# Agent attention and a gated convolution on one core: TensorE's opening steps in a written order, a query load behind the values, value products in 32-column tiles

## The chip, the cores and the metric

One core of a Trainium2 chip runs the kernel. The metric is the device time of one execution in microseconds (us). The engines are TensorE (PE in the profile; its weight loads are PEld), VectorE (DVE), ScalarE (ACT), GpSimd (POOL) and SyncE (SP), which here only issues transfers.

## What is computed

Four batches, 12800 positions, 128 channels, 49 agents. The agents attend to all keys and gather the values; every query then attends to the agents; the result goes through a causal five-tap gate, a value product and an output product.

```python
def sm(a, b):
    s = scale * (a @ b.transpose(0, 2, 1))
    s = s - s.max(-1, keepdims=True)
    e = np.exp(s)
    return e / (e.sum(-1, keepdims=True) + 1e-09)
agent_v = sm(agents, k) @ v
x = sm(q, agents) @ agent_v
...
for k in range(K):
    gate_pre += conv_w[k][None, None, :] * xp[:, k:k + S, :]
gate = 1.0 / (1.0 + np.exp(-gate_pre))
val = x @ w_val
return (gate * val @ w_out).astype(np.float32)
```

## The kernel before

Positions are cut into 10 units of 1280 for each batch, and into 25 chunks of 512 for the second half. The kernel never forms x: it folds `agent_v` into the convolution and value weights, and applies these to the normalised query scores, which stand with agents on partitions in `x1`.

The names of the steps, used all through this text (b is the batch, u the unit, t the chunk, counted over all batches):

- **k b.u** (`key_scores`): eight float32 products of 32 columns by 320 (L363), written to one of two PSUM buffers `sc`; ScalarE copies them out (L389), VectorE takes the largest (L398). The four products of a half stand at the array's columns 0, 32, 64 and 96.
- **m0 and m1** (`key_max`, two steps each): the largest score of every agent; without it no exponential of the values can start.
- **v b.u** (`agent_values`): exponentials on ScalarE (L455), a block transpose on VectorE (L373), and ten float32 products of 64 columns by 129 (L463), alternating between columns 0 and 64. All units of a batch add up in the PSUM buffer `av`.
- **f1 to f5** (`fold_weights`, five steps in a row): f1 sums and normalises (`av` copied at L491, products L494 and L498, VectorE to `avT` at L508), f2 is a small product (L536), f3 eight transposes of the finished gate and value weights (L593, result `stat`), f4 one transpose (L629), f5 two (L655, result `wo16`). Between them VectorE, ScalarE and GpSimd do the scalings.
- **q b.u** (`queries`): the same eight products as k (L363), then a block transpose (L373), a maximum (L679), a subtraction on GpSimd (L684), exponentials on ScalarE (L692), sums and a scaling on VectorE (L697 to L706), and a split into float16 halves on ScalarE and GpSimd (L713 to L726).
- **t b.u** (`transposes`): the query weights to `x1`. For the first four units TensorE does it with ten transposes (L757), ScalarE and VectorE copy one half each (L764, L769); later units go by DMA. Behind it `shifts` copies five shifted pieces to `x2` by DMA (L791); for the very first unit ScalarE's queue issues two of the five.
- **g t, a t, o t** (`gates`, `values`, `project`): six, two and three float16 products of 128 columns by 512 (L828 and L832, L855 and L859, L898 to L900) in one PSUM bank each (`gate`, `val`, `out`).

The list `work` (L943 to L989) holds the steps in program order, and that is TensorE's order. For the other engines `Plan.order` picks, by estimated costs and the longest tail of work behind each step, what runs next. Loads of 640 KB go through a ring of 11 buffers `ld`, in the order in which `work` uses them; SyncE's queue issues them and most other transfers, strictly one after the other. The agents' table `ag_sb` is that queue's first transfer, the weights `moe` its second (L257, L326).

In `work` before the change stand ten keys, both key-maximum steps, q0.0 and q0.1, ten value units with t0.0 behind the eighth, then f1, k1.0, f2, k1.1, f3, two more keys, chunk 0, and so on with chunks and units in turn.

Of the kernel before, what the change touches and what calls it, by code (L numbers as in the profile page):

```python
# [19 lines left out]
BLK = 32  # L20
AP_ = 64

UNIT = 1280
NBLK = 10
# [17 lines left out]
EARLY = ((1, 4), (2, 5), (4, 6))  # L42
SINGLE = 4
KEYS_EARLY = 2
KEYS_FIRST = 2
AV0 = 4
PE_FIRST = 4
PE_TURNS = ()
TURN = 3
Q_FIRST = 2  # L50
W_AT = 2
T_AT = 7
HOP = 0.09
BACKLOG = 3.0
LANES = 8
# [7 lines left out]
class Plan:  # L63
# [11 lines left out]
    def add(self, engine, us, fn, reads=(), writes=(), moved=0.0, key=None, urge=0.0):  # L75
        i = len(self.steps)
        need = set()
        for x in reads:
            need |= self.wrote.get(x, set())
        for x in writes:  # L80
            need |= self.wrote.get(x, set()) | self.read.get(x, set())
        for x in reads:
            self.read.setdefault(x, set()).add(i)
        for x in writes:
            self.wrote[x], self.read[x] = {i}, set()
        self.steps.append((engine, us, fn, need, moved, key))
        self.urge.append(urge)
# [84 lines left out]
def tile_agent_attention_gated_conv(  # L172
# [9 lines left out]
    nc = tc.nc  # L182
    B, C, N = qT.shape
    A = 49
    NU = N // UNIT
# [4 lines left out]
    VW = NBLK * (C + 1)  # L190
    HB = NBLK // 2
# [4 lines left out]
    add = plan.add  # L196
# [60 lines left out]
    nc.sync.dma_start(out=ag_sb, in_=agT.rearrange("b c a -> c b a"))  # L257
    make_identity(nc, ident)
    make_identity(nc, ident16)
    nc.vector.tensor_tensor(  # L260
# [88 lines left out]
    def load(kind, b, u):  # L349
        i = taken[0] % NLOAD  # L350
        taken[0] += 1
        slot_of[kind, b, u] = i
        if kind == "v":
            dst, src = ld[i], vP[b, u].rearrange("p n c -> p (n c)")
        else:
            dst = ld[i][:, 0:UNIT]
            src = (kT if kind == "k" else qT)[b, :, u * UNIT : (u + 1) * UNIT]
        add("dma", 0.4, lambda: nc.sync.dma_start(out=dst, in_=src), (), [("ld", i)], 1.57)

    def score_matmuls(b, src, out):  # L360
        for j in range(2):
# [17 lines left out]
    def key_scores(b, u):  # L379
        i = slot_of["k", b, u]  # L380
        ps, at = bank()
        km = ("kmx", b % 2)
        add("pe", 1.07, lambda: score_matmuls(b, ld[i], ps), [("ld", i)], [at], key="sc")
# [64 lines left out]
    def agent_values(b, u):  # L448
        e, et = es[u % 2], ets[u % 3]
        i = slot_of["v", b, u]  # L450
        vt = ld[i].rearrange("p (n c) -> p n c", c=C + 1)

        def exps():
            for j in range(2):
                nc.scalar.activation(  # L455
                    out=e[:, j], in_=ks[:, u, j], func=AF.Exp,
                    bias=kbias[b % 2][:, j : j + 1], scale=SCALE,
                )

        def matmuls():  # L460
            for n in range(NBLK):
                o = (n % 2) * AP_
                nc.tensor.matmul(  # L463
                    out=av[o : o + AP_, 0 : C + 1], lhsT=et[:, n, :], rhs=vt[:, n, :],
                    start=(u == 0 and n < 2), stop=(u == NU - 1 and n >= NBLK - 2),
                )
# [3 lines left out]
        add(  # L470
            "pe", 1.07, matmuls, [("eT", u % 3), ("ld", i)], ["av"], key="av"
        )


    av2 = const.tile([P, C + 1], F32, name="av2")
# [191 lines left out]
    def queries(b, u):  # L667
        g = b * NU + u
        x = g % 2
        i = slot_of["q", b, u]  # L670
        ps, at = bank()
        sT, d, e, w, r, sm = sts[x], qw[g % 3], qw[g % 3], qw[g % 3], qr[x], qsm[x]
        pt = pts[g % 3]
        sa = sT[:, :, 0:A]
        add("pe", 1.07, lambda: score_matmuls(b, ld[i], ps), [("ld", i)], [at], key="sc")
# [26 lines left out]

        add("dve", 0.95, sums, [("qw", g % 3)], [("qr", x)])
        add(
            "dve", 0.68,
            lambda: nc.vector.tensor_tensor(  # L706
                out=w, in0=e, in1=r.unsqueeze(2).to_broadcast([P, NBLK, A]), op=ALU.mult
            ),
            [("qw", g % 3), ("qr", x)], [("qw", g % 3)],
        )  # L710
# [13 lines left out]
        add(  # L724
            "pool", 1.09,
            lambda: nc.gpsimd.tensor_tensor(  # L726
                out=pt[:, :, A : 2 * A], in0=w, in1=pt[:, :, 0:A], op=ALU.subtract
            ),
            [("qw", g % 3), (*p_, 0)], [(*p_, 1)],
        )  # L730
# [219 lines left out]
    work += [("fold", 0), ("k", 1, 0), ("fold", 0), ("k", 1, 1), ("fold", 0)]  # L950
    after = {
        0: [("fold", 0), ("q", 0, 2), ("fold", 0), ("t", 0, 1), ("q", 0, 3)],
        1: [("t", 0, 2)],
        2: [("t", 0, 3)],
    }
    before = {t: [] for t in range(NT + 2)}
# [5 lines left out]
    for b in range(B):  # L962
        t0 = b * NCH
        for i in range(NU):
            g = b * NU + i + LEAD
            if EARLY[-1][1] < g < B * NU:
                before[t0 + at[i]].append(("q", g // NU, g % NU))
                behind[t0 + at[i] + 2].append(("t", g // NU, g % NU))
        if b + 1 < B:
            u0 = KEYS_FIRST if b == 0 else KEYS_EARLY  # L970
            part = (NU - u0 + 3) // 4
            for n, u in enumerate(range(u0, NU)):
                before[t0 + at[n // part]].append(("k", b + 1, u))
            for t in MAX_AT:
                behind[t0 + t].append(("max", b + 1))
            for u in range(NU):
                before[t0 + at[AV0 + u // 2]].append(("v", b + 1, u))
            for i in range(5):
                behind[t0 + at[AV0 + 4] + i].append(("fold", b + 1))
            if b + 2 < B:  # L980
                for u in range(KEYS_EARLY):
                    before[t0 + at[NU - 1]].append(("k", b + 2, u))
    for t in range(len(chunks) + 2):
        work += before.get(t, [])
        if t < len(chunks):
            work += [("g", t), ("a", t)] + after.get(t, [])
        if t >= 2:
            work.append(("o", t - 2))
        work += behind.get(t, [])  # L989

    loads = [w for w in work if w[0] in "qkv"]

# [65 lines left out]
```

## Time and profile before

| | |
|---|---|
| median of 3 runs (lowest to highest) | 431.86 us (431.13 to 434.68) |
| the profiled execution, its own time | 431.22 us |
| its span | 429.4 us |
| TensorE busy within the span | 402.9 us |
| VectorE, ScalarE, GpSimd busy | 297.0, 300.4, 224.3 us |
| mean granted clock of TensorE | 0.996 |

How to read it: a row of the timeline gives the start, the length, the engine, the line, the operation with its output and inputs, the tile of the array, the shape and the count of merged instructions; in brackets stands how long the engine had been idle before it and whose end released it. TensorE's instructions overlap, so the length of a row holds the last one's tail, and the step from one row's start to the next one's is the better measure. A wait of TensorE is time at the end only while TensorE is the engine that sets the end.

### The profile page before, as it was taken

What the parts mean: (1) busy time and instruction counts of PE and PEld (TensorE: products, weight loads), DVE (VectorE), ACT (ScalarE), POOL (GpSimd) and SP (SyncE); (2) the same over time, 40 slices, a digit from 0 to 9 for tenths busy, and PEclk for the clock granted to TensorE, in tenths of its full rate; (3) what the DMA queues carried; (4) which work ended last, traced back from release to release, by engine and by line L of the source; (5) the groups of instructions that cost most, each with busy time, mean ns of one, the idle gap of its engine ahead of it and who ended that gap; (6) DMA issues with size and microseconds to landing.
All of it is one profiled execution on the core that took longest, in us unless ns stands there. A gap on an engine that the chain in (4) does not pass through costs nothing.

```text
span 429.4 us, 8968 instructions
## 1 busy us (share of the span) xinstructions
PE 402.9 (94%) x3307; PEld 194.8 (45%) x3307; DVE 297.0 (69%) x555; ACT 300.4 (70%) x520; POOL 224.3 (52%) x239
## 2 busy tenths in 40 slices
PE   3978888999999999999999999999999999999995
PEld 1357333345565444444555544445555544434443
DVE  3776879886786877578666887678666787566231
ACT  1464536678976577778876676778876577777875
POOL 1002246564466665544557665553356466687553
PEclk9999989999999999999999999999999999999999
DMA  8999999999999999999999999999999999887743
GB/s 288 422 415 415 371 350 337 297 285 309 343 358 294 249 270 289 307 309 305 340 329 356 292 323 292 320 312 334 306 330 257 289 291 287 215 199 173 192 156 122
DMA packets 76158, 128.07 MB, mean 298 GB/s; under 512 B 51644, under 2 KB 51900, under 8 KB 76116
## 3 DMA queue, kind: packets, MB, share of 16 engines
q1 hardware_dynamic: 76056, 127.41, 96.0%
q8 instruction: 26, 0.43, 0.4%
q14 instruction: 16, 0.13, 0.1%
q10 hardware_dynamic: 60, 0.10, 0.1%
HBM read 79.25 MB, written 26.21 MB: 246 GB/s over the span
## 4 chain that ended last, share of the span: by engine, by line
PE 65%; DMA 13%; DVE 12%; ACT 5%; issue 3%; SPq 1%; POOL 1%; DVEq 0%; ACTq 0%; POOLq 0%
PE gate L828 20%; PE sc L363 13%; PE av L463 6%; PE gate L832 4%; PE val L855 4%; PE val L859 4%; PE out L898 4%; PE out L899 4%; PE out L900 4%; DMA ld<-qT 3%; DMA ld<-vP 3%; DVE h L868 2%; ACT e L455 2%; DMA ld<-kT 2%; DMA outT<-ob 2%
## 5 line engine op out<-in xcount | busy, mean ns | idle before, releaser
L879 POOL TENSOR_TENSOR hl<-h,hh 128x512 f16<-128x512 f32 (+1 forms) x101 | 117.0, 1160 | 121.3 <-ACT hh L874 113.7
L828 PE MATMUL gate<-x,stat 128*128 128x512 f16 (+1 forms) x500 | 124.4, 378 | 2.4 <-ACT th L841 2.3
L868 DVE SCALAR_TENSOR_TENSOR h<-th,val 128x512 f32<-128x512 f32 x100 | 67.7, 677 | 69.1 <-PE out L899 46.1
L363 PE MATMUL sc<-ld,ag_sb 128*32 128x320 f32 x1280 | 102.0, 452 | 10.0 <-DMA ld<-kT 8.0
L912 ACT ACTIVATE ob<-out,oscale 128x512 f32<-128x512 f32 x98 | 67.2, 686 | 23.5 <-PE out L900 17.4
L841 ACT ACTIVATE th<-gate,unscale 128x512 f32<-128x512 f32 x100 | 68.3, 683 | 19.7 <-PE gate L832 18.0
L828 PEld LDWEIGHTS <-stat 128*128 128x128 f16 x505 | 45.6, 97 | 66.4 <-issue 19.0
L874 ACT CAST hh<-h 128x512 f16<-128x512 f32 (+1 forms) x101 | 61.4, 608 | 13.1 <-DVE h L868 12.4
L684 POOL TENSOR_TENSOR qw<-sT,qmx 128x490 f32<-128x490 f32 x40 | 41.5, 1038 | 50.2 <-DVE qmx L679 50.1
L363 PEld LDWEIGHTS sc<-ld,ag_sb 128*32 128x32 f32 x1280 | 37.0, 112 | 62.8 <-issue 22.5
L463 PE MATMUL av<-ld,eT 128*64 128x129 f32 x800 | 49.5, 275 | 1.7 <-DMA ld<-vP 1.4
L389 ACT COPY ks<-sc 128x640 f32<-128x640 f32 x40 | 27.7, 691 | 32.7 <-PE sc L363 30.6
L463 PEld LDWEIGHTS av<-ld,eT 128*64 128x64 f32 x800 | 43.7, 136 | 11.7 <-issue 7.3
L726 POOL TENSOR_TENSOR pt<-qw,pt 128x490 f16<-128x490 f32 x40 | 44.7, 1119 | 3.8 <-ACT pt L713 3.1
L455 ACT ACTIVATE e<-ks,kbias 128x320 f32<-128x320 f32 x80 | 39.0, 553 | 6.1 <-DVE kbias L444 3.3
L373 DVE STREAM_TRANSPOSE eT<-e 128x640 f32<-128x640 f32 x40 | 33.6, 842 | 11.4 <-ACT e L455 5.9
L373 DVE STREAM_TRANSPOSE sT<-sc 128x640 f32<-128x640 f32 x40 | 33.3, 834 | 10.8 <-PE sc L363 10.6
L398 DVE TENSOR_REDUCE kmx<-ks 128x2 f32<-128x640 f32 x39 | 31.4, 817 | 11.8 <-ACT ks L389 11.8
L832 PE MATMUL gate<-x,stat 100*128 100x512 f16 x100 | 38.0, 380 | 0.8 <-DMA x<-x 0.8
L855 PE MATMUL val<-x,stat 128*128 128x512 f16 x100 | 37.8, 378 | 0.1
L859 PE MATMUL val<-x,stat 100*128 100x512 f16 x100 | 37.8, 378 | 0.0
L898 PE MATMUL out<-hh,wo 128*128 128x512 f16 x98 | 37.1, 379 | 0.0
(125 smaller groups left out, 392.1 us busy)
## 6 DMA issues: line engine op xcount, KB each, us to landing
ld<-vP SPq DMA_DIRECT2D x40, 645.0 KB
ld<-kT SPq DMA_DIRECT2D x40, 640.0 KB
ld<-qT SPq DMA_DIRECT2D x40, 640.0 KB
outT<-ob SPq DMA_DIRECT2D x48, 512.0 KB
x<-x SPq DMA_DIRECT2D x90, 100.0 KB
x<-x SPq DMA_DIRECT2D x18, 50.0 KB
outT<-ob SPq DMA_DIRECT2D x3, 256.0 KB
x<-pt SPq DMA_TRANSPOSE x36
```

The costliest lines, as they stand in the source:

```text
L363: nc.tensor.matmul(out=out[g * BLK : (g + 1) * BLK, j, 0:GT], lhsT=ag_sb[:, b, j * BLK : (j + 1) * BLK], rhs=src[:, g * GT : (g + 1) * GT] ...
L373: nc.vector.transpose(out=out.rearrange("p n (j i) -> p j n i", j=2), in_=in_.rearrange("p j (n i) -> p j n i", i=BLK),)
L463: nc.tensor.matmul(out=av[o : o + AP_, 0 : C + 1], lhsT=et[:, n, :], rhs=vt[:, n, :], start=(u == 0 and n < 2), stop=(u == NU - 1 and n >= ...
L828: nc.tensor.matmul(out=pg, lhsT=stat[:, k, :], rhs=x1[:, c : c + w], start=(k == 0), stop=False,)
L832: nc.tensor.matmul(out=pg, lhsT=stat[0 : TAPS * X2R, TAPS + 1, :], rhs=x2[0 : TAPS * X2R, o2 : o2 + w], start=False, stop=True,)
L841: lambda: nc.scalar.activation(out=th, in_=pg, func=AF.Tanh, scale=unscale[:, 0:1]),
L855: nc.tensor.matmul(out=pv, lhsT=stat[:, TAPS, :], rhs=x1[:, PAD + n0 : PAD + n0 + w], start=True, stop=False,)
L859: nc.tensor.matmul(out=pv, lhsT=stat[0 : TAPS * X2R, TAPS + 2, :], rhs=x2[0 : TAPS * X2R, o2 : o2 + w], start=False, stop=True,)
L868: lambda: nc.vector.scalar_tensor_tensor(out=h, in0=th, scalar=1.0, in1=pv, op0=ALU.add, op1=ALU.mult),
L874: "act", 0.16 + 0.42 * scale, lambda: nc.scalar.copy(out=hh, in_=h),
L879: lambda: nc.gpsimd.tensor_tensor(out=hl, in0=h, in1=hh, op=ALU.subtract),
L912: lambda: nc.scalar.activation(out=ob[:, o : o + w], in_=po, func=AF.Copy, scale=oscale),
```

## The change

- `Q_FIRST` goes from 2 to 1: q0.1 is no longer loaded ahead of the values but behind them, and computed behind f1.
- t0.0 moves from between v0.7 and v0.8 (`T_AT` 10 switches that place off) to behind f1.
- The last value unit of batch 0, v0.9, is loaded in two halves with a key each (`ld`, `ld2`), and its products are two steps, one for each half.
- Every product of 64 columns in `agent_values` becomes two of 32 columns, at the array's columns 0, 32, 64 and 96; its step carries the same key as the scores.
- The order of all steps up to o14 is written out. `KEYS_FIRST` moves the units k1.2 and k1.3 into it.
- The agents' table is laid out on the host as it stands on the chip, so that a partition reads one row of 1024 bytes instead of four of 256, and ScalarE's queue issues it instead of SyncE's.

The diff, cut to its core:

```diff
-Q_FIRST = 2
+Q_FIRST = 1
-T_AT = 7
+T_AT = 10
...
-    nc.sync.dma_start(out=ag_sb, in_=agT.rearrange("b c a -> c b a"))
+    nc.scalar.dma_start(out=ag_sb, in_=agT)
...
+        parts = [(dst, src, [("ld", i), ("ld2", i)])]
+        if (kind, b, u) == ("v", 0, NU - 1):
+            h = VW // 2
+            parts = [(dst[:, 0:h], src[:, 0:h], [("ld", i)]), (dst[:, h:], src[:, h:], [("ld2", i)])]
...
-                nc.tensor.matmul(
-                    out=av[o : o + AP_, 0 : C + 1], lhsT=et[:, n, :], rhs=vt[:, n, :],
-                    start=(u == 0 and n < 2), stop=(u == NU - 1 and n >= NBLK - 2),
-                )
+                for j in range(0, AP_, BLK):
+                    nc.tensor.matmul(
+                        out=av[o + j : o + j + BLK, 0 : C + 1],
+                        lhsT=et[:, n, j : j + BLK], rhs=vt[:, n, :],
+                        start=(u == 0 and n < 2), stop=(u == NU - 1 and n >= NBLK - 2),
+                        tile_position=(0, o + j),
+                    )
...
+    order = (
...
+        "v0.5 v0.6 v0.7 v0.8 v0.9 f0 t0.0 q0.1 f0 f0 k1.0 f0 k1.1 q0.2 g0 k1.2 f0 t0.1 a0 q0.3 "
+        "k1.3 q0.4 k1.4 g1 t0.2 q0.5 a1 g2 k1.5 o0 a2 t0.3 t0.4 g3 a3 o1 q0.6 g4 o2 a4 t0.5 "
...
+    )
+    first = [(kinds.get(x[0], x[0]), *map(int, x[1:].split("."))) for x in order.split()]
+    for w in first:
+        work.remove(w)
+    work = first + work
```

What stands on the queues now, at the places that matter below. (`f0` in the written order is the next step of the fold of batch 0. Line numbers of the changed kernel are 8 to 20 higher: L371 is L363, L473 is L463, L777 is L757, L613 is L593. A number behind a name is the buffer: `ld_71` holds v0.9 before; after, `ld_70` holds v0.9 and `ld_71` q0.1.)

TensorE from the last value unit to the first chunk, before:

```order
L463 MATMUL av<-ld_71,eT_82 64x129 x10
L494 MATMUL out<-fold,av_157 128x64
L498 MATMUL out<-fold,av_157 128x64
L363 MATMUL sc_128<-ld_61,ag_sb 32x320 x8
L536 MATMUL val<-avT,moe_sb 128x49
L363 MATMUL sc_129<-ld_62,ag_sb 32x320 x8
L593 LDWEIGHTS wst_118
L593 MATMUL gate<-ident_137,wst_118 128x128
...
L363 MATMUL sc_128<-ld_63,ag_sb 32x320 x8
L363 MATMUL sc_129<-ld_64,ag_sb 32x320 x8
```

The same place now:

```order
L473 MATMUL av<-ld_70,eT_82 32x129 x20
L514 MATMUL out<-fold,av_157 128x64
L518 MATMUL out<-fold,av_157 128x64
L777 LDWEIGHTS pt_96
L777 MATMUL sc_128<-ident_137,pt_96 128x128
...
L371 MATMUL sc_129<-ld_71,ag_sb 32x320 x8
L556 MATMUL val<-avT,moe_sb 128x49
L613 LDWEIGHTS wst_118
L613 MATMUL gate<-ident_137,wst_118 128x128
...
L371 MATMUL sc_128<-ld_61,ag_sb 32x320 x8
```

Before, two key units stood between f1 and f3, one ahead of f2 and one behind it; now t0.0 and q0.1 stand ahead of f2, nothing stands between f2 and f3, and the keys come behind f3.

ScalarE from the split of q0.0 to the weights' copies (`wst`) that f3 reads, before:

```order
L713 CAST pt_96<-qw_89 128x10x49
L764 COPY x_99<-sc_129 128x640
L791 DMA x_100<-x_99 20x1280 x2
L692 ACTIVATE qw_90<-qw_90 128x490
L389 COPY ks<-sc_128 128x640
L579 COPY wst_118<-wst_118 128x5x49
L389 COPY ks<-sc_129 128x640
L583 COPY wst_118<-wst_118 128x49
```

And now:

```order
L733 CAST pt_96<-qw_89 128x10x49
L784 COPY x_99<-sc_128 128x640
L599 COPY wst_118<-wst_118 128x5x49
L811 DMA x_100<-x_99 20x1280 x2
L603 COPY wst_118<-wst_118 128x49
L628 COPY stat_120<-gate 128x512
L397 COPY ks<-sc_128 128x640
L712 ACTIVATE qw_90<-qw_90 128x490
```

The two transfers of `shifts` that ScalarE issues stood ahead of the fold; they now stand between its two copies of the weights.

VectorE around the same weights now (before, the copy to `x1` stood ahead of L491):

```order
L588 TENSOR_SCALAR wst_118<-gw,rs 128x5x49
L789 COPY x_99<-sc_128 128x640
L568 SCALAR_TENSOR_TENSOR wst_118<-gw,rs,wst_118 128x5x30
L568 SCALAR_TENSOR_TENSOR wst_118<-gw,rs,wst_118 128x5x19
L574 TENSOR_REDUCE mx<-val 128x1
L578 TENSOR_SCALAR mx<-mx 128x1
L582 RECIPROCAL rs<-mx 128x1
L583 TENSOR_SCALAR wst_118<-val,rs 128x49
```

The copy of t0.0's second half to `x1` (L789) now stands inside the fold's chain, ahead of the value weights.

More of the change, by code (lines that the diff above doesn't have):

```diff
@@ L357, in load @@
             src = (kT if kind == "k" else qT)[b, :, u * UNIT : (u + 1) * UNIT]
-        add("dma", 0.4, lambda: nc.sync.dma_start(out=dst, in_=src), (), [("ld", i)], 1.57)
+        parts = [(dst, src, [("ld", i), ("ld2", i)])]
+        if (kind, b, u) == ("v", 0, NU - 1):
+            h = VW // 2
+            parts = [(dst[:, 0:h], src[:, 0:h], [("ld", i)]), (dst[:, h:], src[:, h:], [("ld2", i)])]
+        for d, f, keys in parts:
+            add(
+                "dma", 0.4, lambda d=d, f=f: nc.sync.dma_start(out=d, in_=f), (), keys,
+                1.57 / len(parts),
+            )
     def score_matmuls(b, src, out):
@@ L458, in exps, with matmuls @@
                 )
-        def matmuls():
-            for n in range(NBLK):
+        def matmuls(blocks):
+            for n in blocks:
                 o = (n % 2) * AP_
-                nc.tensor.matmul(
-                    out=av[o : o + AP_, 0 : C + 1], lhsT=et[:, n, :], rhs=vt[:, n, :],
-                    start=(u == 0 and n < 2), stop=(u == NU - 1 and n >= NBLK - 2),
-                )
+                for j in range(0, AP_, BLK):
[5 more added lines that the diff above has]
+                    )
         add("act", 1.0, exps, [("ks", u), ("kbias", b % 2)], [("e", u % 2)])
         add("dve", 0.84, lambda: transpose_blocks(et, e), [("e", u % 2)], [("eT", u % 3)])
-        add(
-            "pe", 1.07, matmuls, [("eT", u % 3), ("ld", i)], ["av"], key="av"
-        )
+        h = HB if (b, u) == (0, NU - 1) else NBLK
+        first = range(0, h)
+        add(
+            "pe", 1.07 * h / NBLK, lambda: matmuls(first),
+            [("eT", u % 3), ("ld", i)] + [("ld2", i)] * (h == NBLK), ["av"], key="sc",
+        )
+        if h < NBLK:
+            add(
+                "pe", 1.07 * (1 - h / NBLK), lambda: matmuls(range(h, NBLK)),
+                [("eT", u % 3), ("ld2", i)], ["av"], key="sc",
+            )
     av2 = const.tile([P, C + 1], F32, name="av2")
@@ L949, in tile_agent_attention_gated_conv @@
             work.append(("t", 0, 0))
-    work += [("fold", 0), ("k", 1, 0), ("fold", 0), ("k", 1, 1), ("fold", 0)]
+    work += [("fold", 0), ("t", 0, 0), ("q", 0, 1), ("fold", 0), ("k", 1, 0), ("fold", 0), ("k", 1, 1), ("q", 0, 2), ("fold", 0)]
     after = {
-        0: [("fold", 0), ("q", 0, 2), ("fold", 0), ("t", 0, 1), ("q", 0, 3)],
-        1: [("t", 0, 2)],
+        0: [("fold", 0), ("t", 0, 1), ("k", 1, 2), ("q", 0, 3)],
+        1: [("k", 1, 3), ("t", 0, 2)],
         2: [("t", 0, 3)],
@@ L972, in tile_agent_attention_gated_conv @@
             for n, u in enumerate(range(u0, NU)):
-                before[t0 + at[n // part]].append(("k", b + 1, u))
+                before[t0 + at[n // part + (b == 0)]].append(("k", b + 1, u))
             for t in MAX_AT:
@@ L989, in tile_agent_attention_gated_conv @@
         work += behind.get(t, [])
+    kinds = {"m": "max", "f": "fold"}
+    order = (
[6 rows of a table added]
+    )
+    first = [(kinds.get(x[0], x[0]), *map(int, x[1:].split("."))) for x in order.split()]
+    for w in first:
+        work.remove(w)
+    work = first + work
     loads = [w for w in work if w[0] in "qkv"]
@@ L1029, in words @@
         return w.view(np.int64) if w.dtype == np.float64 else w
-    agT = np.zeros((b, c, AP_), agents.dtype)
-    agT[:, :, :a] = agents.transpose(0, 2, 1)
+    agT = np.zeros((c, b, AP_), agents.dtype)
+    agT[:, :, :a] = agents.transpose(2, 0, 1)
     vP = np.ones((b, nu, P, NBLK, c + 1), v.dtype)
```

6 lines of the change are left out of this document (3 added, 3 removed), and 4 rows, old and new, of the table order.

## The prediction

> **What bounds the kernel now.** I read the page's busy lines first, then TensorE's waits from 88 us on, then its timeline ahead of that, and last the other engines where it waits.
>
> ```profile
> PE 402.9 (94%) x3307; PEld 194.8 (45%) x3307; DVE 297.0 (69%) x555; ACT 300.4 (70%) x520; POOL 224.3 (52%) x239
> ```
>
> ```profile
> PE sc L363 <- DVE sT L373: 1.9, 3, 0.8
> PE gate L828 <- ACT th L841: 1.6, 5, 0.6
> PE gate L832 <- DMA x<-x: 0.8, 1, 0.8
> ```
>
> TensorE is busy for 94% of the span, and behind 88 us its largest wait is 1.9 us in all, in three pieces: there only fewer or shorter TensorE instructions shorten the kernel. Room is in the first 88 us. TensorE's timeline shows the places:
>
> ```profile
> 36.27 1.32 PE L463 MATMUL av<-ld,eT 128*64 128x129 f32 x20 [0.26 <-DMA ld<-vP]
> 39.22 0.73 PE L757 MATMUL sc<-ident,pt 128*128 128x128 f16 x10
> 39.89 2.58 PE L463 MATMUL av<-ld,eT 128*64 128x129 f32 x40
> 42.85 0.43 PE L494 MATMUL out<-fold,av 128*128 128x64 f32 x2 [0.39 <-DVE av L491]
> 43.44 1.28 PE L363 MATMUL sc<-ld,ag_sb 128*32 128x320 f32 x16
> 44.65 0.42 PE L536 MATMUL val<-avT,moe_sb 128*128 128x49 f32 x2
> 45.01 1.28 PE L363 MATMUL sc<-ld,ag_sb 128*32 128x320 f32 x16
> 47.43 0.61 PE L593 MATMUL gate<-ident,wst 128*128 128x128 f16 x8 [1.14 <-DVE wst L548]
> 55.42 0.23 PE L655 MATMUL val<-ident,wsp 128*128 128x128 f16 x1 [1.92 <-DVE wsp L642]
> 56.53 3.87 PE L363 MATMUL sc<-ld,ag_sb 128*32 128x320 f32 x32
> 62.86 3.99 PE L363 MATMUL sc<-ld,ag_sb 128*32 128x320 f32 x48
> 69.90 0.73 PE L757 MATMUL sc<-ident,pt 128*128 128x128 f16 x10 [1.21 <-POOL pt L726]
> 84.12 1.24 PE L828 MATMUL gate<-x,stat 128*128 128x512 f16 x5 [0.71 <-ACT th L841]
> 86.60 2.36 PE L363 MATMUL sc<-ld,ag_sb 128*32 128x320 f32 x32
> 89.25 1.28 PE L363 MATMUL sc<-ld,ag_sb 128*32 128x320 f32 x16 [0.29 <-DVE sT L373]
> 92.97 1.24 PE L828 MATMUL gate<-x,stat 128*128 128x512 f16 x5
> ```
>
> Until 42.47 (39.89 + 2.58) the loads set the pace: a value unit takes 1.32 us and then 0.26 pass until the next load is there, a step of 1.58. Then the fold and the first chunks make TensorE wait. At 56.53 two score units take 3.87 us where two at 86.60 take 2.36; three windows show that stretch, the one ahead of it, and a later one:
>
> ```profile
> 53.80:57.20 3.40, 1.62 (x24) 1.11 (x28) 2.58 (x8) 0.62 (x2) 1.95 (x2) 1.00 1.03 426
> 57.20:60.60 3.40, 3.40 (x29) 0.92 (x21) 2.90 (x6) 1.35 (x3) 0.65 (x2) 0.50 1.01 417
> ...
> 72.00:80.00 8.00, 8.00 (x75) 3.13 (x77) 7.85 (x13) 6.29 (x12) 4.95 (x6) 1.00 1.09 314
> ```
>
> Behind the window's length stand the busy times of TensorE, its loads, VectorE, ScalarE and GpSimd; the third number from the end is the granted clock. After 3.4 us in which TensorE was busy for 1.62, its clock stood at half for the next 3.4. And from 72 to 80 VectorE is as full as TensorE.
>
> From 42.47 to chunk 8 (the 92.97 row) I count as lost: 0.39 ahead of f1, 1.14 ahead of f3, 1.92 ahead of f5, 1.51 at half clock (3.87 less 2.36), 0.55 in the three units at 62.86 (3.99 less 2.36 and 1.08; one unit more adds 2.36 less 1.28, that is 1.08), 1.21 ahead of t0.3, 0.71 and 0.29. In all 7.7 us. Chunk 8 is a good mark: at it the two orders have done the same work.
>
> **The change, part by part.** *The end of the values.* One load less ahead of them gives 1.58. The table's transfer leaves SyncE's queue, and all behind it can be issued earlier by its place there:
>
> ```profile
> 0.74 0.47 SPq L257 DMA_DIRECT2D ag_sb<-agT  x1
> 1.26 0.49 SPq L326 DMA_DIRECT2D ob<-moe  x1
> ```
>
> That is 0.52 (1.26 less 0.74). It is nothing if the engines that move the data, and not the queue, set the start; I take 0.52, since nothing is under way when the queue begins. On ScalarE, which now issues it, it delays the table of functions, and that is hidden: ScalarE has nothing to do before the first scores. The last load in halves lets half of v0.9 be done while the other half is under way: half of 1.10 (2.42 less 1.32, rows here and below), 0.55. Sum: 2.65 earlier, so the values end at 39.8. What feeds them keeps up with the loads:
>
> ```profile
> L455 ACT ACTIVATE e<-ks,kbias 128x320 f32<-128x320 f32 x80 | 39.0, 553 | 6.1 <-DVE kbias L444 3.3
> L373 DVE STREAM_TRANSPOSE eT<-e 128x640 f32<-128x640 f32 x40 | 33.6, 842 | 11.4 <-ACT e L455 5.9
> ```
>
> Two exponentials are 1.11 us a unit and a transpose 0.84, both below 1.58.
>
> *Work that comes behind it.* q0.1 (1.08) and t0.0 (0.67: 39.89 less 39.22) lay in the loads' shadow and now lie on the path. The written order also alternates more between tile sizes: by the order six switches more from the values' end to chunk 8, at 0.09 each (next paragraph), 0.5. Together +2.2.
>
> *The tiles.* Rows where units stand between other sizes:
>
> ```profile
> 97.79 0.38 PE L900 MATMUL out<-hl,wo 128*128 128x512 f16 x1
> 98.09 0.70 PEld L363 LDWEIGHTS sc<-ld,ag_sb 128*32 128x32 f32 x16 [0.42 <-issue]
> 98.09 1.28 PE L363 MATMUL sc<-ld,ag_sb 128*32 128x320 f32 x16
> 99.31 2.42 PE L463 MATMUL av<-ld,eT 128*64 128x129 f32 x40
> 101.67 1.25 PE L828 MATMUL gate<-x,stat 128*128 128x512 f16 x5
> ```
>
> From L900 to the unit pass 0.30, where products of 128 columns follow each other at 0.22 (1.24 less 0.38 for four steps, the 92.97 row): 0.08 for the switch. From the scores to the values pass 1.22, not 1.08: 0.14. Two value units take 2.36 from start to start, 2.20 and 0.16 for both ends. With 32-column tiles the switch between scores and values goes. By the order there are ten switches fewer behind chunk 20, and between chunks 8 and 20 as many as before, one more or less. Bounds 0.8 (0.08 each) and 1.4 (0.14); I take 1.0, nearer to the plain switch. The streaming itself I leave as it is: four products of 32 columns side by side are as much as two of 64. That the array does run four side by side the scores show:
>
> ```profile
> L363 PE MATMUL sc<-ld,ag_sb 128*32 128x320 f32 x1280 | 102.0, 452 | 10.0 <-DMA ld<-kT 8.0
> ```
>
> One after the other, 1280 of 452 ns would be 579 us; they were busy for 102.
>
> *The waits.* What f3 needed, before:
>
> ```profile
> 40.72 0.49 DVE L769 COPY x<-sc 128x640 f16<-128x640 f16 x1 [0.75 <-ACT x L764]
> 41.24 2.08 ACTq L791 DMA_DIRECT2D x<-x  x2
> 44.29 0.21 DVE L508 TENSOR_TENSOR avT<-out,den 128x49 f32<-128x49 f32 x1
> 45.30 0.47 DVE L568 TENSOR_SCALAR wst<-gw,rs 128x245 f16<-128x245 f32 x1
> 46.95 0.23 ACT L583 COPY wst<-wst 128x49 f16<-128x49 f16 x1
> ```
>
> Now `avT` ends at 41.85 (44.50 less 42.47 behind the values' end, as before) and the gate weights at 43.1 (45.77 less 44.50 later). The x1 copy follows on VectorE until 43.6; it releases the two transfers on ScalarE's queue, 2.08 long, until 45.7; the copy of the value weights is queued behind them, 0.23; f3 starts at 46.0. From 40.2 TensorE does f1, t0.0, q0.1 and f2 (0.59, 0.67, 1.21 and 0.36 from the rows' starts), is done at 43.0 and waits **3.0 us**, where it waited 1.14. A stretch like the one at 53.8 arises, so I expect the half clock again, somewhere from 46 to 50, for 1.5. On the other side k1.1, q0.2, chunk 0 and k1.2 now stand between f4 and f5, so the 1.92 goes, and t0.1's and t0.2's data are begun earlier against their place. What is late next is a transpose in VectorE's full queue: q0.4 needs the `sc` buffer of q0.3, whose transpose is queued behind the sums of q0.2, and these wait for GpSimd, which splits q0.1 first. Bounds: nothing, if VectorE catches up during the 3.0, and the 1.21 that t0.3 waited at such a place; I take 0.7. So 0.4 (f1) + 3.0 + 1.5 + 0.7 = 5.6 instead of 7.7, **2.1 less**.
>
> The three transfers of `shifts` on SyncE go out from 43.6 on (before, 41.24, with the ones on ScalarE), and k1.3 is the first load behind them; TensorE uses it at about 56, so nothing waits. The load of q0.1 lands a step of 1.58 behind the values', about 40.6, and is used at 41.5: 0.9 of cover, and if that is gone, q0.1 slips into the wait for f3, which has 3.0.
>
> Sum: −2.65 + 2.2 − 2.1 − 1.0 = −3.55. The profiled execution took 431.22: **427.7 us**. The median of the runs was 431.86, 0.64 above it; so this is 0.8% under the profiled execution and 1.0% under the median.
>
> **The rivals.** *TensorE can't be fed (slower).* A value unit becomes 40 loads and 40 products. Before, two units with 80 of them took 2.36 us, 29 ns each. If that is the fastest TensorE takes them, a unit lasts 2.36: the first ten, paced at 1.58, lose 0.8 each, 30 more 1.18: +43, 471 us. It decides from 16 ns on (3.55 us over 30 units are 0.12; 1.18 + 0.12 over 80). Against it: at 98.09 sixteen loads pass in 0.70, with products among them. [...] Chance 0.08.
>
> *The fold's wait eats it.* The half clock lasts two stretches (1.5 more), and GpSimd holds up VectorE where both run:
>
> ```profile
> L706 DVE TENSOR_TENSOR qw<-qw,qr 128x490 f32<-128x490 f32 x40 | 34.7, 868 | 0.4
> 67.35 0.67 DVE L706 TENSOR_TENSOR qw<-qw,qr 128x490 f32<-128x490 f32 x1
> ```
>
> 0.2 over the mean of eight query units is 1.6, most of it on the chain that holds q0.4 and its like. Then 427.7 + 1.5 + 1.4 = 430.6. Chance 0.20.
>
> *The clock stays up and VectorE keeps pace.* Less 1.5 and 0.7: 425.5. For it: a wait of 3.0 is a little shorter than a stretch. [...] The 53.80 row is against it: half idle was enough. Chance 0.16.
>
> *The tiles change nothing* (TensorE drains between scores and values all the same): 428.7. Chance 0.07.
>
> **How the numbers follow.** My forecast has 0.49, with a range of its own of 426.2 to 429.2; the rivals 0.08, 0.20, 0.16 and 0.07. About 1% is what a measurement of this kernel can tell from no change, and 427.5 is that bound below the median. Half of my forecast's chance lies under it, 0.25; with the third rival that is 0.41 faster. The other half, the second and the fourth make 0.51 the same, the first 0.08 slower. Range 425.0 to 430.9: outside are the slow rival and the ends of the others.
>
> **What the profile would show.** Right: the values' last product ends near 39.8; f3 starts near 46 behind a wait of about 3; no wait at f5; a stretch at half clock behind it; chunk 8 starts near 90.4; behind it a value unit starts 1.1 after a score unit. Wrong: value units longer than 1.3 us, f3 without that wait, waits over 1 us around q0.4 and t0.2, or transfers late for q0.1 or chunk 0.

## The result, and the profile after

The changed kernel is slower by 0.8%: 436.53 us median (433.4 to 442.27, 22 runs) beside 432.44 (429.76 to 435.64, 22 runs), a ratio of 1.0079 with a 95% interval of 1.0055 to 1.0104. The forecast was 427.7 with a range of 425.0 to 430.9. Executions in a disturbed, slower state stand in these medians but are left out of every ratio here, and e5 has no ratio because only two of its six were left.

The profiled execution took 433.97. Its busy lines, from the page of the changed kernel:

```profile
span 432.2 us, 10568 instructions
PE 402.8 (93%) x4107; PEld 196.9 (46%) x4107; DVE 297.8 (69%) x555; ACT 300.4 (70%) x520; POOL 225.6 (52%) x239
```

TensorE does 800 products more in the same busy time, and the span is 2.8 us longer: the time went into waits. The opening on TensorE's timeline:

```profile
5.66 3.96 PE L371 MATMUL sc<-ld,ag_sb 128*32 128x320 f32 x28 [5.66 <-DMA ld<-kT]
...
25.72 11.11 PE L473 MATMUL av<-ld,eT 128*32 128x129 f32 x292 [1.03 <-DVE eT L381]
39.02 3.28 PE L473 MATMUL av<-ld,eT 128*32 128x129 f32 x108 [2.18 <-issue]
42.69 0.43 PE L514 MATMUL out<-fold,av 128*128 128x64 f32 x2 [0.39 <-DVE av L511]
...
43.84 0.73 PE L371 MATMUL sc<-ld,ag_sb 128*32 128x320 f32 x5
45.30 1.27 PE L371 MATMUL sc<-ld,ag_sb 128*32 128x320 f32 x11 [0.73 <-issue]
...
48.54 0.34 PE L613 MATMUL gate<-ident,wst 128*128 128x128 f16 x3 [1.34 <-ACT wst L603]
...
52.58 1.25 PE L848 MATMUL gate<-x,stat 128*128 128x512 f16 x5
```

The first scores start 1.44 earlier than before (7.10), but the values end at 42.30 (39.02 + 3.28), where they ended at 42.47 and should have ended at 39.8. Two rows carry a wait for "issue", 2.18 and 0.73: TensorE stood still with nothing to wait for that the profile shows. The f3 wait is there (1.34), 6.2 behind the values' end as forecast.

The windows view (busy times, then granted clock, DMA share and GB/s at the end), the changed kernel:

```profile
25.00:43.00 18.00, 14.70 (x403) 13.67 (x403) 11.10 (x17) 9.72 (x20) 2.56 (x3) 0.82 1.03 415
43.00:60.00 17.00, 14.91 (x173) 6.45 (x175) 15.08 (x41) 7.88 (x14) 4.95 (x7) 1.00 0.85 323
150.00:250.00 100.00, 95.77 (x1006) 46.80 (x1005) 71.15 (x130) 72.47 (x127) 53.65 (x56) 1.00 1.03 309
250.00:350.00 100.00, 97.59 (x993) 47.62 (x992) 72.87 (x133) 73.20 (x128) 56.55 (x58) 1.00 1.04 310
```

and the kernel before:

```profile
150.00:250.00 100.00, 98.81 (x822) 47.85 (x819) 73.25 (x135) 74.34 (x129) 56.13 (x59) 1.00 1.04 310
250.00:350.00 100.00, 98.68 (x802) 47.90 (x801) 72.45 (x132) 73.97 (x129) 55.20 (x57) 1.00 1.05 307
```

From 150 to 350 TensorE is busy for 4.1 us less than before, and in both kernels the transfer engines have a share of 1.03 to 1.05, that is, by this measure they are full. The waits there (in all, number, longest), the changed kernel and then the kernel before:

```profile
ACT ob L932 <- DMA outT<-ob: 12.4, 6, 3.3
PE gate L848 <- ACT th L861: 5.7, 7, 1.7
ACT pt L733 <- DMA x<-pt: 3.7, 5, 1.2
```

```profile
ACT ob L912 <- DMA outT<-ob: 2.5, 1, 2.5
PE gate L828 <- ACT th L841: 0.8, 3, 0.3
```

ScalarE waits for output stores to free an `ob`, so its next `th` is late, and TensorE's next gate waits for that. Where the lead goes shows in the starts of the chunks, read off TensorE's timeline as each chunk's first gate product (chunks are counted from 0 to 100, the last two half as long; a sign means us against the profiled execution of the kernel before; runs e7 to e18 are below):

| kernel | chunk 0 | 8 | 24 | 64 | 100 | from 24 to 80 |
|---|---|---|---|---|---|---|
| before | 50.26 | 92.97 | 155.34 | 313.21 | 421.99 | 215.86 |
| changed | +2.32 | -3.07 | -2.03 | +2.86 | +2.73 | 220.19 |
| e13: changed, large tiles in batch 0 | +1.09 | -4.42 | -4.68 | +3.60 | +3.47 | 223.97 |
| e7: before, 20 loads less | -0.34 | -0.75 | -0.75 | -0.97 | -2.54 | 214.22 |
| e18: as e13, 20 loads less | -0.40 | -5.78 | -6.05 | -6.95 | -9.01 | 213.05 |

Each row is one execution, and executions of one kernel differ by some us, so the rows are read together with the ratios. The changed kernel's own row is a lucky one. Runs e1 and e8 below have the same steps in the same order up to chunk 8, and they reach it at 92.95 and 95.14, that is 0.02 ahead and 2.17 behind, where this one was 3.07 ahead; in them the values end at 44.08 and 44.91. Behind the stall for "issue" their clock stood at half for 3.4 us, and here it did not. Two stretches around that stall, e1 and then the changed kernel:

```profile
36.70:40.10 3.40, 0.97 (x36) 0.97 (x40) 1.59 (x4) 0.61 (x1) 1.49 (x2) 1.00 1.02 414
40.10:43.50 3.40, 3.40 (x73) 3.32 (x68) 0.00 (x0) 0.00 (x0) 0.05 (x1) 0.50 1.03 417
```

```profile
34.90:38.30 3.40, 1.93 (x68) 1.66 (x60) 3.09 (x7) 1.83 (x4) 0.00 (x0) 1.00 1.04 410
38.30:41.70 3.40, 2.69 (x99) 2.69 (x103) 0.24 (x1) 0.61 (x1) 1.54 (x2) 1.00 1.03 420
```

### The profile page after: what moved, and what is told of

The parts are those of the page before. It is cut to its first block, busy times and chain, and to the rows that moved or that the text cites. A ratio compares the mean times of both kernels' runs of the same rounds, so it can differ in the third digit from the quotient of the medians.

```text
span 432.2 us, 10568 instructions
## 1 busy us (share of the span) xinstructions
PE 402.8 (93%) x4107; PEld 196.9 (46%) x4107; DVE 297.8 (69%) x555; ACT 300.4 (70%) x520; POOL 225.6 (52%) x239
## 4 chain that ended last, share of the span: by engine, by line
PE 62%; DMA 17%; ACT 7%; DVE 6%; issue 3%; SPq 2%; POOL 2%; ACTq 0%; DVEq 0%
PE gate L848 18%; PE sc L371 12%; PE av L473 10%; DMA outT<-ob 7%; DMA x<-pt 5%; DMA ld<-kT 4%; PE val L875 4%; PE gate L852 3%; PE val L879 3%; PE out L918 3%; PE out L919 3%; PE out L920 3%; ACT e L463 2%; SPq L811 2%; ACT th L861 2%
## 5 line engine op out<-in xcount | busy, mean ns | idle before, releaser
L371 PE MATMUL sc<-ld,ag_sb 128*32 128x320 f32 x1280 | 101.1, 446 | 9.1 <-DMA ld<-kT 6.7
L371 PEld LDWEIGHTS sc<-ld,ag_sb 128*32 128x32 f32 x1280 | 36.6, 111 | 61.8 <-issue 22.9
L473 PE MATMUL av<-ld,eT 128*32 128x129 f32 x1600 | 50.4, 283 | 3.2 <-issue 2.2
L473 PEld LDWEIGHTS av<-ld,eT 128*32 128x32 f32 x1600 | 46.8, 114 | 9.3 <-issue 3.3
L746 POOL TENSOR_TENSOR pt<-qw,pt 128x490 f16<-128x490 f32 x40 | 45.9, 1149 | 2.5 <-ACT pt L733 1.9
L463 ACT ACTIVATE e<-ks,kbias 128x320 f32<-128x320 f32 x80 | 39.4, 553 | 6.8 <-DVE eT L381 3.9
L406 DVE TENSOR_REDUCE kmx<-ks 128x2 f32<-128x640 f32 x39 | 31.5, 815 | 13.4 <-ACT ks L397 13.4
```

Of the source, the lines that this page charges most:

```text
L371: nc.tensor.matmul(out=out[g * BLK : (g + 1) * BLK, j, 0:GT], lhsT=ag_sb[:, b, j * BLK : (j + 1) * BLK], rhs=src[:, g * GT : (g + 1) * GT] ...
L473: nc.tensor.matmul(out=av[o + j : o + j + BLK, 0 : C + 1], lhsT=et[:, n, j : j + BLK], rhs=vt[:, n, :], start=(u == 0 and n < 2), stop=(u ...
```

## Experiments

**The order of SyncE's queue.** Behind chunk 20 TensorE, VectorE, ScalarE and GpSimd have their steps in the same order in both kernels; on SyncE's queue 66 of 207 transfers changed places, since `Plan.order` timed everything anew. In e1 and e2 the list of steps is written out, with that queue's part exchanged:

```diff
-    for i in plan.order():
+    for i in map(int, order.split()):
         plan.steps[i][2]()
```

> The changed kernel, but with SyncE's transfers behind chunk 20 in the order that they had before the change; every other queue as it is. Theory 1 (the new order of that queue makes output stores and transposes late, and TensorE waits for them): the 5.1 us that the changed kernel lost behind chunk 20 come back, ratio to before 0.996 (0.993 to 0.999), and ScalarE's waits for the output stores fall from 15.9 us to about 4. Theory 2 (the transfers as a whole are full, so that whatever lead the opening wins is given back later, in any order): ratio stays near 1.008 and the waits of ScalarE stay above 10 us.

Measured: 1.0104 (1.0054 to 1.0155). The old order did not help the changed kernel; theory 1 falls as far as the order alone is to be the cause, and e1 is not told apart from the changed kernel itself (1.0079).

> The kernel before, but with SyncE's transfers behind chunk 20 in the changed kernel's order; nothing else. Theory 1 (that order costs the time): slower by about 5 us, ratio 1.012 (1.008 to 1.015), with chunk 20 where it was and the loss behind it. Theory 2 (the lead is given back whatever the order): no lead, nothing to give back, ratio 1.000 (0.997 to 1.003).

Measured: 1.0059 (1.0031 to 1.0088). In the kernel before the new order does cost 2.5 us, half of what theory 1 gave and more than theory 2 gave, and the waits of the changed kernel appear from 150 to 350, this kernel's:

```profile
ACT ob L912 <- DMA outT<-ob: 9.8, 3, 3.8
PE gate L828 <- ACT th L841: 4.7, 6, 1.8
```

So the new order costs under the old opening, and the old order does not help under the new one; e15 shows on what the cost depends.

**The tiles.** e3 is the kernel before with the loop over 32-column tiles of the change; e4 is the changed kernel without it:

```diff
-                for j in range(0, AP_, BLK):
+                nc.tensor.matmul(out=av[o : o + AP_, 0 : C + 1], lhsT=et[:, n, :], ...)
```

> The kernel before with only the value products cut into tiles of 32 columns; every queue's order as before. Theory 3 (the doubled number of TensorE's instructions makes it stall for instructions while the loads are at their densest): value phase loses 1 to 3 us at the stalls, which idle marked as issue shows, and the switches saved behind it win 1.4: ratio 0.998 to 1.003. Rival (the stalls have another cause): no stalls above 0.3 us between 25 and 43 us, and the saved switches make it 0.996 to 0.997.

> The changed kernel with the value products in tiles of 64 columns as before; every queue's order as in the changed kernel. Theory 3 (twice the instructions make the stalls): the stalls of 2.2 and 0.7 us between 25 and 47 us are gone, the values end near 40.1, the fold and chunk 0 start 2 us earlier, and behind chunk 20 about 1 us is lost for the switches; ratio 1.003 to 1.008. Rival: stalls remain with half the instructions, the values end near 42, ratio 1.009 to 1.012.

Measured: e3 1.0147 (1.0105 to 1.019), worse than either theory gave (in its profiled execution 3.9 us are lost by chunk 8 and 7.5 by the end); e4 1.0018 (0.9984 to 1.0052). The values on e3's timeline:

```profile
33.97 3.73 PE L464 MATMUL av<-ld,eT 128*32 128x129 f32 x127 [0.27 <-issue]
40.12 1.52 PE L464 MATMUL av<-ld,eT 128*32 128x129 f32 x44 [2.43 <-issue]
...
46.36 0.43 PE L464 MATMUL av<-ld,eT 128*32 128x129 f32 x8 [1.94 <-issue]
```

and on e4's:

```profile
25.73 13.90 PE L471 MATMUL av<-ld,eT 128*64 128x129 f32 x200 [0.87 <-DVE eT L381]
40.01 0.43 PE L510 MATMUL out<-fold,av 128*128 128x64 f32 x2 [0.38 <-DVE av L507]
```

With large tiles the values end at 39.63 and no stall is left. What TensorE waits for is, as read from the packets below, its own code. The page's queue of instructions, before and changed:

```profile
q8 instruction: 26, 0.43, 0.4%
```

```profile
q8 instruction: 32, 0.52, 0.5%
```

Each of these packets has 16384 bytes. Their times in the packet records, beside TensorE's records (products, weight loads and semaphore instructions) counted from the start:

```
kernel   packet on the wire   TensorE stops after record   stands still
changed  36.46 to 37.49        961                         36.56 to 39.01
changed  42.78 to 43.78       1217                         44.13 to 45.30
e3       31.65 to 32.75        705                         33.43 to 33.97
e3       37.78 to 38.88        961                         37.42 to 40.12
e3       43.89 to 44.97       1217                         44.16 to 46.36
e1       30.28 to 31.38        705                         30.83 to 32.72
e1       36.75 to 37.85        961                         36.18 to 39.13
before   35.05 to 36.14        705                         (reached at 38.33, no stall)
```

Where a kernel with small tiles in batch 0 stops, it stops at the same records, 256 apart, and the stop ends 1.2 to 1.5 us behind the packet. In these openings a packet starts only when the block before it has been begun, and among the loads, at these stops, mostly 3.5 to 4.0 us later (32.94 to 36.46 and 39.01 to 42.78 in the changed kernel, 32.72 to 36.75 in e1); with 1.05 on the wire and 1.3 behind it that is about 6 us. A value unit is 80 records now, so 256 last 5.1 us at the loads' pace (3.2 units by 1.58) and less where TensorE catches up; before, 40 records a unit made it 10, which was enough even where 6.6 us passed until the packet (28.44 to 35.05). The number of packets goes with the records: 26 for TensorE's 6717 before, 32 for its 8320 now, 258 and 260 for each packet. At such a stop TensorE stands idle for up to 2.7 us (e1, ahead of 39.13).

**Transfers that stand ahead of loads.** In the changed kernel SyncE issues no load from 37.07 to 48.55, behind the copies of t0.0, and the packet records show the transfer engines on average more than half empty from 45.8 to 49.6 (share 0.39, and 0.85 in the row above for the 17 us around it). e5 puts these copies behind two loads:

```diff
 load q0.3
-shifts of t0.0 (3 transfers)
 load k1.3
 load q0.4
+shifts of t0.0 (3 transfers)
```

> The changed kernel, with the three transfers of t0.0 on SyncE's queue moved behind the loads of k1.3 and q0.4, and nothing else. Theory 4 (the transfer engines are as full as TensorE all through, so that a stretch in which they stand empty is paid for at the end): the 2.7 us in which they stand empty between 45.8 and 49.6 shrink below 0.7, chunk 0 comes up to 1 us later, and the kernel as a whole gains about 2, ratio 1.002 to 1.005. Rival (TensorE alone sets the end): nothing on TensorE's path needs those loads early, and chunk 0 waits for the later copies, ratio 1.008 to 1.012.

No ratio came of it; its six executions took 430.18 to 441.53, so neither theory is decided. Its profile shows the empty stretch moved, not gone: the share is 0.95 from 43 to 60, and now 0.91 from 60 to 90:

```profile
43.00:60.00 17.00, 14.73 (x152) 6.08 (x155) 13.77 (x39) 7.10 (x12) 4.51 (x6) 0.90 0.95 365
60.00:90.00 30.00, 30.00 (x277) 12.28 (x269) 27.34 (x48) 23.18 (x39) 20.91 (x22) 1.00 0.91 289
```

**The table alone.** The two lines on `agT` of the change, in the kernel before.

> The kernel before with only the agents' table on ScalarE's queue, laid out on the host as it stands on the chip. The first scores start 1.4 us earlier. Theory 4: the loads begin 1.4 us earlier and are never empty in the opening, so the lead stays to the end, ratio 0.995 to 0.998. Rival (a lead of the opening is lost behind it whatever its cause): 0.999 to 1.002.

Measured: 0.9982 (0.9952 to 1.0012): 0.8 us or nothing. The first scores start at 6.20, 0.9 earlier.

**Room on the transfer engines.** The light runs leave loads out:

```diff
         slot_of[kind, b, u] = i
+        if kind in "kq" and b >= 2 and u % 2:
+            return
```

> The kernel before without the loads of the odd key and query units of batches 2 and 3 (those units compute on what the buffers hold): 20 loads, 31 us of transfers less, all other work as before. Theory 4: with room on the transfer engines ScalarE's waits for the output stores behind 150 us go, ratio 0.985 to 0.993. Rival (TensorE alone sets the end): 0.997 to 1.000.

> The changed kernel without the same 20 loads. Theory 4: what the change lost behind chunk 20 was lost to the transfers, so now it keeps its lead of the opening and the saved tile switches, and is faster than the kernel before without these loads by 2 to 4 us. Rival (the loss behind chunk 20 is on the engines, by the order or by the tiles): still slower than that kernel by 2 to 5 us.

Without these loads the units compute on old data. Measured: e7 0.9954 (0.9924 to 0.9984), e8 0.9944 (0.9908 to 0.998). Taking 31 us of transfers away (20 loads, a step of 1.58 each) gains the kernel before only 2.0 us, less than theory 4 gave: the full transfers cost the kernel before little. But the 0.79% between the two kernels is gone. That e8 is not faster than e7 is its opening, with the stalls and the half clocks in it: its chunk 24 starts 2.93 later than e7's, and of that 1.77 is left at chunk 80. From 150 to 350 neither ScalarE nor a product of TensorE waits for a transfer in e8 or e7 (weight loads do, for 1.3 and 2.0 us in all, and GpSimd once or twice for 3.5). All that TensorE's products wait for there in e7:

```profile
PE sc L365 <- DVE sT L375: 0.8, 1, 0.8
PE gate L830 <- ACT th L843: 0.6, 2, 0.3
PE av L631 <- ACT stat L610: 0.3, 1, 0.3
```

**Longer rings.** `NOB = 4` in both kernels, and with `w = AP_ if b == 0 else BLK` as the tiles' width in e11 (large tiles in batch 0).

> The changed kernel with four output buffers `ob` instead of three, every queue's order as it is. Theory 5 (behind chunk 20 the loss comes from output stores that land late behind the loads and copies ahead of them, so that ScalarE waits for a free `ob` and TensorE for ScalarE): ScalarE's 15.9 us of waits for stores fall below 4, TensorE's 7.0 us of waits for `th` below 3, and 3 to 5 us come back, ratio 0.997 to 1.001. Rival (full transfer engines hold up something else as soon as this wait is gone): ratio 1.004 to 1.009, with TensorE waiting for `x2` or loads in its place.

> The kernel before with four output buffers `ob`, orders as they are. Its profile shows 4.1 us of ScalarE's waits for stores and 1.6 us of TensorE's for `th`. Theory 5: at most those 1.6 us and some of what the slower executions lose, ratio 0.994 to 0.999. Rival: 0.999 to 1.002.

> The changed kernel with four output buffers and with 64-column tiles for the values of batch 0 alone, 32-column tiles in the other three batches. Theories 3 and 5 together: no stall for instructions between 25 and 47 us, values end at 39.6, saved tile switches kept behind chunk 20, no wait for stores: ratio 0.990 to 0.995, faster than both kernels. If only theory 3 holds: 0.998 to 1.003.

Measured: e9 1.0054 (1.0015 to 1.0092), e10 1.003 (0.9996 to 1.0063), e11 0.9997 (0.9961 to 1.0033), which is what theory 3 alone gave. Theory 5 falls: e9 and e10 stay above its ranges. The wait for stores goes and others come, in e10 from 150 to 350 (before, the first was 0.6 and the second was not there):

```profile
ACT pt L713 <- DMA x<-pt: 6.9, 2, 3.8
PE av L419 <- DVE m L412: 1.7, 1, 1.7
```

**Which part needs the room.** Small tiles in batches 1 to 3 alone, in the kernel before (`w = AP_ if b == 0 else BLK`); the same without the 20 loads; and e2 without them.

> The kernel before with 32-column tiles for the values of batches 1 to 3 alone; all orders as before. Theory 3 (the small tiles hurt by the stalls for instructions in the opening and only there): the opening as before, 1.1 to 1.4 us saved at tile switches later, ratio 0.996 to 0.998. Rival (the small tiles also cost behind the opening, as the 3.3 us that the kernel with small tiles alone lost behind chunk 40 suggest): 1.003 to 1.009.

> The kernel before with small tiles in batches 1 to 3 and without the 20 loads of batches 2 and 3; to be held against the kernel before without these loads, 0.9954. Theory 4 (the small tiles cost only because the transfer engines have no room): the saved tile switches show, 1.1 to 1.4 us, ratio 0.991 to 0.994. Rival (the small tiles cost by themselves): 0.998 to 1.002.

> The kernel before with SyncE's transfers behind chunk 20 in the changed kernel's order and without the 20 loads. Theory 4 (the order costs only where the transfer engines have no room): ratio 0.994 to 0.997, like the kernel before without these loads. Rival (the order costs by itself, by stores and copies that stand behind waiting transposes): 0.999 to 1.003.

Measured: e12 1.0043 (1.0008 to 1.0078), e14 0.9918 (0.9886 to 0.995), e15 0.9944 (0.9919 to 0.9969). With all loads both parts cost; without the 20 loads neither does. (Against e7's 0.9954, e14 is 0.4% lower and e15 0.1%; the intervals overlap.) From chunk 24 to chunk 80 e7 takes 214.22, e15 214.23, e14 213.07: there the new order costs nothing, and the small tiles save 1.15 us. So neither has a cost of its own that shows here; each costs only while all loads are there. That it is the transfer engines' time is read from their share, 1.03 to 1.05 in both kernels with all loads and 0.87 to 1.00 without the 20; the light runs also take 20 entries off SyncE's queue, and no run separates the two.

**Three units on TensorE.** As e13 (large tiles in batch 0), and

```diff
-PE_TURNS = ()
-TURN = 3
+PE_TURNS = (0,)
+TURN = 9
```

> The changed kernel with 64-column tiles for the values of batch 0 alone, three output buffers. Theory 3: values end at 39.6 and not 42.3, 2 to 3 us of the loss go, ratio 1.000 to 1.003. Rival (whatever the opening wins is given back behind it): 1.005 to 1.009, with chunk 24 earlier by 2 us or more than in the changed kernel and chunk 64 not.

> As the run with 64-column tiles in batch 0 alone, and three of the 36 units that a transfer transposes (the first of each of three groups, in batches 0, 1 and 2) are transposed by TensorE: 7.2 us of transfers less (2.4 each, from 46080 packets of 256 bytes that take 86 us of all sixteen engines), 2.2 us of TensorE more. Theory 4: the room pays for it or nearly, ratio lower than without it by 0 to 0.4%. Rival (TensorE sets the end): higher by 0.5%.

Measured: e13 1.003 (0.9999 to 1.0061), e16 1.0045 (1.0015 to 1.0076). e13's ratio is at the edge of theory 3's range, but its chunks do what the rival said: chunk 24 starts 2.65 earlier than in the changed kernel, and chunk 64 does not (the table). The two intervals overlap, and the exchange gains nothing that can be seen. In e16 `Plan.order` set the order of all queues from about q0.6 on anew, so it is not the exchange alone that was measured.

**The last two.** e17 is e11 with `pts = ring(4, ...)`; e18 is e13 without the 20 loads.

> The changed kernel with 64-column tiles in batch 0, four output buffers and four buffers `pt` of query weights, orders as they are. With four output buffers alone ScalarE still waited 8.2 us for transposes to free a `pt`. If those waits are what is left: they go, TensorE's waits for `th` fall from 5.1 to below 3, ratio 0.994 to 0.998. If full transfer engines move the wait on once more: 0.998 to 1.002, with waits for `x2` or for loads.

> The changed kernel with 64-column tiles in batch 0 and without the 20 loads of batches 2 and 3; to be held against the kernel before without these loads, 0.9954. Theory 4: chunk 24 starts 4 to 5 us earlier than in that kernel and the lead stays and grows by the saved tile switches: ratio 0.981 to 0.987. Rival (a lead is given back even with room): 0.990 to 0.996.

Measured: e17 1.0036 (0.9994 to 1.0077), e18 0.9779 (0.9735 to 0.9823). In e17 the wait moved once more, on to `x2` and loads:

```profile
PE gate L853 <- DMA x<-x: 4.6, 4, 2.7
PE av L474 <- DMA ld<-vP: 2.9, 6, 1.3
```

e18, with four executions, is 1.8% under e7 (0.9779 over 0.9954), below the range of theory 4. Its windows:

```profile
150.00:250.00 100.00, 98.69 (x1023) 48.46 (x1022) 73.29 (x138) 75.44 (x132) 57.10 (x60) 1.00 0.98 282
250.00:350.00 100.00, 98.98 (x1013) 48.37 (x1012) 73.72 (x135) 75.01 (x130) 56.64 (x59) 1.00 0.91 254
```

With a share of 0.98 and 0.91 instead of 1.03 and 1.04 TensorE stays busy, and the lead of 5.3 us that e18 has over e7 at chunk 24 is 6.5 at chunk 80. With all loads the same program (e13) has 4.7 of lead over the kernel before at chunk 24 and is 3.4 behind it at chunk 80. No kernel that does all the work came out faster than the kernel before by more than its interval.

## Why the prediction was wrong

- **The bound.** The step that failed is the reading that behind 88 us "only fewer or shorter TensorE instructions shorten the kernel", so that a lead at chunk 8 is kept to the end. The third window quoted there had a DMA share of 1.09 beside TensorE's 8.00 busy of 8.00. By these measures TensorE and the transfers were both at their limit, and only one of them was put into the sum. In the profiled execution chunk 8 stands 3.07 ahead, a little more than forecast, and the end 2.73 behind instead of 3.55 ahead: its whole miss of 6.3 us lies behind chunk 8. The median misses by 8.8, and the openings of e1 and e8 show where more can be lost.
- **Term 1, -2.65 to the values' end.** Measured -0.17, and with large tiles -2.84 (e4). That e4's sum agrees is in part luck: the first scores come 1.39 earlier there (5.71) and not 0.52, and so 1.45 is left for the missing load and the halves, which were put at 2.13. The fall in the changed kernel is the stalls for code, 2.18 in the value phase and 0.73 behind it, and in e1 and e8 also the half clock behind a stall of 2.4 to 2.7. The rival "TensorE can't be fed" asked the right question of the wrong thing: products pass fast enough (two value units behind the opening take 2.32, before 2.36), their code does not arrive. The table alone gave 0.9 (e6).
- **Term 2, +2.2, and term 3, -2.1.** Chunk 8 at 89.91 against 90.4 is luck: the values end 2.5 later than forecast, and from there to chunk 8 pass 47.6 and not 50.6, because the wait of f3 was shorter and the half clock behind it (1.5) did not come. The mechanism is right. The f3 wait came as named, 6.2 behind the values, at 1.34 and not 3.0 because the second stall (44.13 to 45.30) and five of the eight transposes, done ahead of it, took part of that time. e4 is nearly the forecast's trace: values' end at 39.63, waits of 0.95 and 1.58 ahead of f3's two parts, the half clock (0.80 from 43 to 60), chunk 8 at 89.72. A half clock ahead of it, unforeseen (0.82 from 25 to 43), cost little where the loads set the pace: e4's values end at 39.63 with it.
- **Copies on SyncE's queue, costed at nothing.** "TensorE uses it at about 56, so nothing waits" is true of TensorE. The transfer engines stood empty instead (0.85). What that alone is worth stays open: e5 moved it and gave no ratio.
- **Term 4, -1.0 for ten switches.** The saving is real (1.15 in e14; in the changed kernel a value unit starts 1.10 behind a score unit, 98.34 less 97.24, as forecast) and is not seen with full transfers (e12 +0.43%).
- **Not in the sum: everything behind chunk 20 but the switches.** The lead of 2.42 at chunk 20 became 2.73 behind at chunk 100. It is shown that this loss goes when 20 loads are left out (e7, e8, e14, e15, e18), so it needs the full load of transfers. Not shown is why a kernel with a lead ends behind one without instead of level with it; that SyncE's order no longer fits the times at which stores, transposes and loads come due is the likeliest reading of e1, e2 and e15, and only argued. In some runs a half clock behind these waits adds to it (e13: 3.4 us at 0.50 from 240.4; e1: 6.8 from 186.9); in the changed kernel's profiled execution there is none behind 31.5 until the last chunk, and it loses 5.15 (2.42 and 2.73) all the same.

## What to carry to other kernels

Read the transfers' share in the same stretches as TensorE's busy time: where both were near 1 (here 1.03 to 1.05, and 0.96 to 0.99), a lead that TensorE had won was no gain until the transfers had room (e13 1.003, e18 0.9779), and a longer ring moved the wait (e10, e17). Test for that bound by leaving some loads out; run with and without the edit, it tells whether the edit has a cost of its own. Before cutting products into smaller tiles, count instructions: here TensorE stopped where 256 records last 5.1 us or less and their refill took about 6 among dense loads, and did not stop in the kernel before, where they last 10 and the refill took 9 (28.44 to 36.14, with 1.3 counted behind it). Where a forecast meets its mark, check the terms too: chunk 8 came right by two misses that cancelled.

## What the runs showed of the hardware

The refill of TensorE's code stands in the packet records beside the loads: in the openings 0.8 to 6.6 us pass between the start of a block and the next packet (e4, 29.66 to 30.44; before, 28.44 to 35.05), then about 1.05 on the wire, and at a stop 1.2 to 1.5 until TensorE goes on. That the loads hold the packet up is not shown. Behind the opening a block lasted long enough even with small tiles: in e3 about 3.5 us or more lie between the end of a packet and its use, by the count of records, and no stall follows.

In the traces of the two kernels every stretch of one granted clock between two changes lasts 3.41 us or a multiple of it: at half 3.41 (before, from 57.23) and 6.83 (the changed kernel, from 24.62), at full 368.64 and 399.36, that is 108 and 117 times 3.41. Counted in such steps from where a half clock begins, the clock was granted at half behind a stretch in which TensorE was busy for about half of it or less, however the idle time was cut up: behind 1.62 of 3.40 (before, from 53.80), 0.97 (e1, from 36.70) and 1.61 (the changed kernel, from 21.20, with waits of 1.26 and 0.62 in it at the key maximum; half from 24.6 to 31.5, the second step behind one that was itself at half, with 2.37 busy). It stayed up behind 1.93 (the changed kernel, from 34.90), 1.90 (from 45.10) and 2.11 (before, from 23.10). So two like stalls differed by how they fell across these stretches: in the changed kernel the stall of 2.45 from 36.56 to 39.01 lies across two of them, and no half clock followed; in e1 the one from 36.18 to 39.13 lies mostly in one, and the next was at half.

What the second rival said of GpSimd and VectorE is partly in the trace of the kernel before: the 40 executions of L706 took 0.63 to 0.67 in all 18 beside which GpSimd stood still, and beside work of GpSimd 0.66 to 0.67 in 7 and 0.76 to 1.51 in 15.
